# Experts' rows turned as float32r and as float32, and expert 0's row loads placed ahead of a branch

## The chip, the cores and the metric

One core of a Trainium2 chip runs the whole program. The metric is the device time in microseconds of one execution; the kernel before has a median of 955.91 us over two timed runs (955.81 and 956.01).

## What is computed

Three layers follow one another: attention with a gate (4 batches, 8 heads, 576 positions, 64 wide), a mixture of 8 experts with one expert per row (2304 rows of 512, 1024 hidden units), and a gated product of two matrices (1536 wide). The part that matters here is the second:

```python
N, D, E, F = (2304, 512, 8, 1024)
expert_idx = np.argmax(logits, axis=1)
...
for e in range(E):
    mask = expert_idx == e
    ...
    h = np.maximum(x[mask] @ w1[e], 0.0)
    out[mask] = gate_w[mask, None] * (h @ w2[e])
```

## The kernel before

Attention runs under a schedule made when the program is built, and its last tiles scatter their rows into a table `xs` in DRAM, one stretch per expert, with indirect DMAs from GpSimd. After that everything stands in the order in which the code issues it; every engine takes its instructions in that order.

Matrix products of float32 accuracy are made of three float32r products: an operand is split into a high half (`xh`, `hh`, the first half of a weight tile `w` or `v`), which is a cast, and a low half (`xl`, `hl`, the second half of the tile), which is the difference; high by high, low by high and high by low are added in PSUM. A weight tile `st` (128 x 1024) comes by SyncE's queue; `hi_op` casts it on ScalarE, `lo_op` subtracts on VectorE ("D") or GpSimd ("G"), 512 columns at a time.

The experts run in order of their size (`CAPS`, 352 to 272 rows; `ARMS` and `narrow` choose a column count of 256 or more by the true count). For expert `e` and each of 8 column blocks `f`, `products` issues 12 matmuls `h` (`hmm`), 12 matmuls `y` of the block before (`ymm`), the ReLU into `hh` on ScalarE and `hl` on VectorE. After the products of `f` = 3 to 6, `xtr(e + 1, f - 3)` turns a quarter of the next expert's rows: three 128x128 transposes into a PSUM bank `x` (two banks in turn), a cast to `xh` on ScalarE, a subtraction to `xl` on VectorE. Each turn also splits one weight tile and loads another (`wsplit2`, `wload2`), and takes one of the small jobs `m1` to `m5` out of `misc`. The rows of an expert come by `xload(e)` into a tile `xg` that has one buffer; `zfill(e)` first writes zeros into the unused rows of its stretch of `xs`. `yout` stores an expert's result `yt` through four buffers of the pool `mxp`, which also serves `g` in the second network.

Between attention and expert 0 stands a hand-over. Every engine reads a count `cov` and branches over a loop (`overflow`) that is for experts that have more rows than planned. TensorE runs warm-up matmuls of 512 columns (`idle(n)`, counts out of `WARM`), SyncE issues `xload(0)` behind the branch, which waits for all scattered rows, VectorE does two `lo_op`s each of tiles 4 and 5 and GpSimd two of tile 6, then `m1` and `m2` (ScalarE and VectorE), `zfill(1)`, three weight loads, and `xtr0` turns expert 0's rows: eight transposes (two row tiles for each of four quarters) and then four, each quarter in its own bank `y`, each followed by a cast and a subtraction.

Of the kernel before, what the change touches and what calls it, by code (L numbers as in the profile page):

```python
# [7 lines left out]
F32 = mybir.dt.float32  # L8
F32R = mybir.dt.float32r
# [4 lines left out]
ALU = mybir.AluOpType  # L14
# [20 lines left out]
PEND = (10, 1, 1)  # L35
WARM = (30, 84, 2, 0, 20, 10, 3)
LAT = 140.0
# [107 lines left out]
def moe_kernel(tc, q, k, v, s, emb, tau, w1, w2, wa, wb, wo, out, dbg=None):  # L145
    nc = tc.nc
# [35 lines left out]
    with left, right:  # L182
# [28 lines left out]
        base = rt.tile([128, E], F32, name="base")  # L211

        pmt = const.tile([128, N // 128, 2], F32, name="pmt")
        cumd = dram.tile([B * H, 64], F32, name="cumd")
# [24 lines left out]

        def slot_load(src):  # L240
            t = slot([128, 1024], F32, "st")
            d = t if len(src.shape) == 2 else t.rearrange("p (a c) -> p a c", a=src.shape[1])
            nc.sync.dma_start(out=d, in_=src)
            return t
# [44 lines left out]
        if True:  # L289
# [839 lines left out]
            def blank(eng, t, n):  # L1129
# [6 lines left out]
                out=ident, in_=onef, pattern=[[-1, 128]], compare_op=ALU.is_equal, fill=0.0, base=0, channel_multiplier=1  # L1136
            )
            nc.gpsimd.memset(mine, -1.0)
            for base_, x in ((0, 1), (31, -1)):
# [201 lines left out]
            hp = pool(right, "hp", 2, side="right")  # L1341
            mxp = pool(right, "mxp", 4, side="right")
            keep = pool(right, "keep", 1, side="right")
# [33 lines left out]
            def xtr0():  # L1377
                t = xhs[0] = [xhp.tile([128, 4, GT], F32R, name=x)[:, :, :CAPS[0]] for x in ("xh", "xl")]
                for a0, a1 in ((0, 256), (256, CAPS[0])):
                    for d in range(4):  # L1380
                        for a in range(a0, a1, 128):
                            nc.tensor.transpose(
                                out=yb[d][:, a:a + 128], in_=xgs[0][:, a // 128, 128 * d:128 * d + 128], identity=ident
                            )
                        nc.scalar.copy(out=t[0][:, d, a0:a1], in_=yb[d][:, a0:a1])
                        nc.vector.tensor_tensor(
                            out=t[1][:, d, a0:a1], in0=yb[d][:, a0:a1], in1=t[0][:, d, a0:a1].bitcast(F32), op=ALU.subtract
                        )

            def xtr(e, d):  # L1390
# [5 lines left out]
                for a in range(3):  # L1396
                    nc.tensor.transpose(  # L1397
                        out=pt[:, 128 * a:128 * a + 128], in_=xgs[e][:, a, 128 * d:128 * d + 128], identity=ident
                    )
                nc.scalar.copy(out=xh[:, d, :], in_=pt[:, :cap])  # L1400
                nc.vector.tensor_tensor(out=xl[:, d, :], in0=pt[:, :cap], in1=xh[:, d, :].bitcast(F32), op=ALU.subtract)

# [19 lines left out]

            def wload2():
                if loaded[0] < len(jobs):
                    key = jobs[loaded[0]][0]
                    stg[key] = slot_load(slot_src(who(key[0]), key[1]))
                    loaded[0] += 1
# [329 lines left out]

            wload2()
            idle(WARM[2])
            most = nc.values_load(cov[:1, 0:1], min_val=-CAP, max_val=N)  # L1760
            overflow()
            xload(0)
            cbase[1] = nc.sync.value_load(ci[:1, 1, 1:2], min_val=0, max_val=N)
            who(1)
            idle(WARM[6])
            count(0)
            for j in range(4, 7):
                for x in range(2):
                    lo_op("DG"[j == 6], wstate[j], slots[0, j], 512 * x, 512 * x + 512)
            for _ in range(2):  # L1770
                misc.pop(0)()
            zfill(1)
            for _ in range(3):
                wload2()
            xtr0()
            prev = None
# [105 lines left out]
```

## Time and profile before

| what | us |
|---|---|
| median of two timed runs | 955.91 |
| profiled execution, its own time | 953.78 |
| span of the profiled execution | 952.1 |
| TensorE busy (share of the span) | 917.8 (96%) |
| VectorE busy | 516.9 (54%) |
| ScalarE busy | 432.0 (45%) |
| GpSimd busy | 256.4 (27%) |

The span runs from the first to the last instruction; the profiled execution's own time is 1.7 us more. Attention takes about 258 us of it, the experts' matmuls run from about 272 to 490 us, the second network from there to the end. A share of busy time is an average over these stages; what a change in one of them is worth is read from that stage. PE in a row is TensorE's matmuls, PEld its weight loads, DVE VectorE, ACT ScalarE, POOL GpSimd, SPq SyncE's queue.

### The profile page before, as it was taken

The page shows a single profiled execution, that of the slowest core. Times are in us where ns is not written, and L with a number is a line of the kernel's source. Part 1 is how long each engine was busy: PE and PEld are TensorE (multiplying, and loading weights), DVE is VectorE, ACT ScalarE, POOL GpSimd, SP SyncE. Part 2 cuts the span into 40 slices and gives each one's busy share as a digit, 9 for nine tenths or more (in the row PEclk, how much of TensorE's full clock was granted, in tenths as well). Part 3 has the DMA queues.
Part 4 walks back from the last instruction along what each step waited for, and adds up shares of the span by engine and source line. Part 5 has one row for each costly group of instructions (what it writes and reads, how often), then busy time and mean ns, then how long its engine had stood idle before and what let it go on. Part 6 is the DMA issues. An engine that isn't in the chain of part 4 may idle for free.

```text
span 952.1 us, 17669 instructions
## 1 busy us (share of the span) xinstructions
PE 917.8 (96%) x6447; PEld 839.7 (88%) x6448; DVE 516.9 (54%) x1319; ACT 432.0 (45%) x1074; POOL 256.4 (27%) x308
## 2 busy tenths in 40 slices
PE   8998999999889999999999999999999999999996
PEld 7777878777669999999998999999999999999995
DVE  8788888798756343455678888732212222222112
ACT  6677888876645444455544434421211111121111
POOL 6122323256234333344303344632001001001001
PEclk9999999999999999999999999999999999999999
DMA  5774555526277667677736444412010010000000
GB/s 136 175 154 105 143 116 123 140 71 185 96 221 241 225 193 218 215 226 241 223 106 204 129 118 131 90 26 75 1 34 34 1 34 34 1 1 34 1 1 34
DMA packets 102259, 107.90 MB, mean 113 GB/s; under 512 B 58445, under 2 KB 72733, under 8 KB 102157
## 3 DMA queue, kind: packets, MB, share of 16 engines
q1 hardware_dynamic: 98573, 97.04, 36.0%
q0 software_dynamic: 3552, 9.46, 2.8%
q8 instruction: 65, 1.06, 0.5%
q14 instruction: 37, 0.30, 0.1%
q10 hardware_dynamic: 32, 0.04, 0.0%
HBM read 77.90 MB, written 20.44 MB: 103 GB/s over the span
## 4 chain that ended last, share of the span: by engine, by line
PE 68%; DMA 2%; DVE 0%; issue 0%; SPq 0%; POOLq 0%; ACT 0%; DVEq 0%; ACTq 0%
PE h L1643 16%; PE x L1643 16%; PE y L1664 14%; PE y L1578 10%; PE h L1553 10%; DMA xg<-xs 1%; PE x L1397 1%; PE x L1664 1%; PE h L1664 1%; DMA xs<-zrow 1%; DMA yt<-mx 0%; DVE xl L1631 0%; SPq L1372 0%; POOLq L1878 0%; DVE mx L1654 0%
## 5 line engine op out<-in xcount | busy, mean ns | idle before, releaser
L1654 DVE TENSOR_TENSOR mx<-x,mx 128x384 f32<-128x384 f32 x72 | 39.9, 555 | 225.1 <-PE x L1643 225.0
L1655 ACT CAST hh<-mx 128x384 fp32r<-128x384 f32 x71 | 36.4, 512 | 159.0 <-DVE mx L1654 159.0
L1649 ACT COPY mx<-h 128x384 f32<-128x384 f32 x72 | 34.5, 479 | 150.8 <-PE h L1643 149.8
L1683 POOL DMA_INDIRECT out_dram<-mx,pmt x18 | 17.6, 979 | 292.5 <-DVE mx L1682 223.2
L653 ACT ACTIVATE z<-z,mn 128x192 f32<-128x192 f32 (+3 forms) x128 | 78.2, 611 | 37.9 <-DVE mn L647 37.2
L1643 PE MATMUL h<-xh,w 128*128 128x384 f32 x288 | 79.8, 337 | 1.3 <-ACT mx L1649 1.3
L1643 PE MATMUL h<-xh,v 128*128 128x384 f32 x288 | 79.7, 337 | 0.0
L1643 PE MATMUL x<-xh,w 128*128 128x384 f32 x288 | 78.9, 334 | 0.0
L633 PE MATMUL st<-KS,QS 128*128 128x288 f32 (+3 forms) x160 | 58.7, 374 | 9.4 <-DVE mn L647 7.4
L756 PE MATMUL pt<-ident,z 128*128 128x128 f32 x448 | 63.5, 277 | 3.3 <-ACT pT L180 1.6
L281 POOL TENSOR_TENSOR w<-st,w 128x512 fp32r<-128x512 f32 (+1 forms) x43 | 47.1, 1101 | 68.1 <-ACT w L273 57.8
L647 DVE CUSTOM_DVE_ANT_0 z<-st,maskb 128x192 f32<-128x192 f32 (+3 forms) x128 | 58.7, 477 | 9.5 <-PE st L636 7.3
L1562 DVE SCALAR_TENSOR_TENSOR hl<-h,hh 128x288 fp32r<-128x288 f32 (+6 forms) x64 | 31.2, 487 | 58.8 <-ACT hh L1561 58.8
L1656 DVE TENSOR_TENSOR hl<-mx,hh 128x384 fp32r<-128x384 f32 x71 | 39.7, 559 | 41.1 <-ACT hh L1655 41.1
L800 PE MATMUL xa<-pT,vn 128*64 128x128 f32 x896 | 60.0, 278 | 1.9 <-ACT pT L180 1.6
L281 POOL TENSOR_TENSOR v<-st,v 128x512 fp32r<-128x512 f32 x32 | 43.2, 1353 | 62.5 <-ACT v L273 48.7
L1664 PE MATMUL y<-v,hh 128*128 128x512 f32 x192 | 59.8, 392 | 0.0
L756 PEld LDWEIGHTS pt<-ident,z 128*128 128x128 f32 x448 | 49.9, 141 | 11.0 <-ACT z L653 4.3
L1553 PE MATMUL h<-xh,v 128*128 128x256 f32 (+2 forms) x256 | 59.0, 304 | 0.0
L1578 PE MATMUL y<-hh,v 128*128 128x256 f32 (+2 forms) x256 | 58.0, 300 | 0.0
L1553 PE MATMUL h<-xh,w 128*128 128x288 f32 (+3 forms) x256 | 57.8, 302 | 0.0
L800 PEld LDWEIGHTS xa<-pT,vn 128*64 128x64 f32 x896 | 47.9, 137 | 11.0 <-issue 5.6
(308 smaller groups left out, 2520.0 us busy)
## 6 DMA issues: line engine op xcount, KB each, us to landing
st<-in_moe_w_dram SPq DMA_DIRECT2D x64, 512.0 KB
QS<-sp SPq DMA_DIRECT2D x62, 128.0 KB
st<-in_moe_w_a_dram SPq DMA_DIRECT2D x12, 512.0 KB
st<-in_moe_w_b_dram SPq DMA_DIRECT2D x12, 512.0 KB
st<-in_moe_w_out_dram SPq DMA_DIRECT2D x12, 512.0 KB
xg<-yt SPq DMA_DIRECT2D x6, 768.0 KB
xg<-xs SPq DMA_DIRECT2D x7, 512.0 KB
kn<-in_k_dram SPq DMA_DIRECT2D x24, 128.0 KB
```

What stands on the lines that cost most here:

```text
L281: e.tensor_tensor(out=o[:, 1, a:b], in0=t[:, a:b], in1=o[:, 0, a:b].bitcast(F32), op=ALU.subtract)
L633: nc.tensor.matmul(st[:m, :wp], lhsT=qs[:, h, s0 - 64:s0 - 64 + m], rhs=ks[:, h, c0:c0 + wp], start=True, stop=False)
L647: nc.vector.tensor_tensor_reduce(out=z[:m, h, c0:c0 + w], in0=st[:m, :w], in1=maskb[:m, S - kk + c0:S - kk + c0 + w], op0=ALU.add, op1=ALU ...
L653: nc.scalar.activation(out=z[:m, h, :kk], in_=z[:m, h, :kk], func=AF.Exp, scale=-1.0, bias=m1, accum_out=rsum[:m, tid(b, c), 2 * p + h:2 * ...
L756: nc.tensor.transpose(out=pt[:, 128 * x:128 * x + 128], in_=zs[i][:, h, a0:a0 + 128] if c else z0s[u % 2], identity=ident)
L800: nc.tensor.matmul(xa[64 * h:64 * h + 64, :m], lhsT=v_[:m, 2 * p + h, :], rhs=locs[i][bk, h], start=bk == 0, stop=bk == c,)
L1553: nc.tensor.matmul(ph[:, :n], lhsT=w[:, hl, 128 * f:128 * f + 128], rhs=mv[:, d, :n], start=k_ == 0, stop=k_ == 11,)
L1578: nc.tensor.matmul(ys[e][d][:, :n], lhsT=w[:, hl, c0 + 128 * d:c0 + 128 * d + 128], rhs=mv[:, :n], start=f == 0 and k_ == 0, stop=f == 7 a ...
L1643: nc.tensor.matmul(p, lhsT=w[:, hl, d, c0:c0 + 128], rhs=mv[:, d, :], start=d == 0 and k_ == 0, stop=d == 3 and k_ == 2,)
L1654: nc.vector.tensor_tensor(out=g, in0=pp[1], in1=g, op=ALU.mult)
L1656: nc.vector.tensor_tensor(out=gl, in0=g, in1=gh.bitcast(F32), op=ALU.subtract)
L1664: nc.tensor.matmul(ots[i][t], lhsT=st[:, 128 * t:128 * t + 128], rhs=w[:, hl, c0:c0 + 512], start=f == 0 and k_ == 0, stop=f == 11 and k_ ...
```

## The change

In `xtr`, the three transposes of a quarter are issued as float32r (rows and a cast identity `idr` taken as float32r), from which `xh` is cast as before; then three more transposes of the same rows are issued as float32 into the other bank `x`. VectorE copies the first result to SBUF (`c1`), subtracts it from the second (`c2`), subtracts `xh` from `c1`, and makes `xl` as `c2` times 1e12 plus that. In `xtr0` the 12 transposes are float32r only. `mxp` has five buffers in place of four.

In the hand-over, `xload(0)` comes before the warm-up and the branch, in the place of the load of weight tile (0, 7); all four warm-up matmuls stand ahead of the branch and none behind it. VectorE keeps the `lo_op`s of tile 4, GpSimd has those of 5 and 6; three small jobs are taken, ahead of GpSimd's `lo_op`s in the code; `xtr0` comes before `zfill(1)` and the weight loads; the load of tile (0, 7) now waits for the ninth transpose of `xtr0`, and two loads follow `zfill(1)` in place of three.

```diff
-WARM = (30, 84, 2, 0, 20, 10, 3)
+WARM = (30, 84, 4, 0, 20, 10, 0)
...
+        idr = const.tile([128, 128], F32R, name="idr")
...
-            nc.sync.dma_start(out=d, in_=src)
+            x = nc.sync.dma_start(out=d, in_=src)
+            if after:
+                tc.add_manual_dep(x.ins, after, DEP, reason="rows first")
...
+            nc.gpsimd.tensor_copy(out=idr, in_=ident)
...
-            mxp = pool(right, "mxp", 4, side="right")
+            mxp = pool(right, "mxp", 5, side="right")
...
-                            nc.tensor.transpose(
-                                out=yb[d][:, a:a + 128], in_=xgs[0][:, a // 128, 128 * d:128 * d + 128], identity=ident
+                            x = nc.tensor.transpose(
+                                out=yb[d][:, a:a + 128].bitcast(F32R), in_=xgs[0][:, a // 128, 128 * d:128 * d + 128].bitcast(F32R), identity=idr
...
+                        if a0 and d == 0:
+                            first = x.ins.name
+                return first
...
-                        out=pt[:, 128 * a:128 * a + 128], in_=xgs[e][:, a, 128 * d:128 * d + 128], identity=ident
+                        out=pt[:, 128 * a:128 * a + 128].bitcast(F32R), in_=xgs[e][:, a, 128 * d:128 * d + 128].bitcast(F32R), identity=idr
                     )
                 nc.scalar.copy(out=xh[:, d, :], in_=pt[:, :cap])
-                nc.vector.tensor_tensor(out=xl[:, d, :], in0=pt[:, :cap], in1=xh[:, d, :].bitcast(F32), op=ALU.subtract)
+                p2 = bank("x")
+                for a in range(3):
+                    nc.tensor.transpose(
+                        out=p2[:, 128 * a:128 * a + 128], in_=xgs[e][:, a, 128 * d:128 * d + 128], identity=ident
+                    )
+                c1, c2 = (mxp.tile([128, 512], F32, name="mx") for _ in range(2))
+                nc.vector.tensor_copy(out=c1[:, :cap], in_=pt[:, :cap])
+                nc.vector.tensor_tensor(out=c2[:, :cap], in0=p2[:, :cap], in1=c1[:, :cap], op=ALU.subtract)
+                nc.vector.tensor_tensor(out=c1[:, :cap], in0=c1[:, :cap], in1=xh[:, d, :].bitcast(F32), op=ALU.subtract)
+                nc.vector.scalar_tensor_tensor(
+                    out=xl[:, d, :], in0=c2[:, :cap], scalar=1e12, in1=c1[:, :cap], op0=ALU.mult, op1=ALU.add
+                )
...
-            wload2()
+            xload(0)
             idle(WARM[2])
             most = nc.values_load(cov[:1, 0:1], min_val=-CAP, max_val=N)
             overflow()
-            xload(0)
+            idle(WARM[6])
             cbase[1] = nc.sync.value_load(ci[:1, 1, 1:2], min_val=0, max_val=N)
             who(1)
-            idle(WARM[6])
             count(0)
-            for j in range(4, 7):
+            for x in range(2):
+                lo_op("D", wstate[4], slots[0, 4], 512 * x, 512 * x + 512)
+            for _ in range(3):
+                misc.pop(0)()
+            for j in (5, 6):
                 for x in range(2):
-                    lo_op("DG"[j == 6], wstate[j], slots[0, j], 512 * x, 512 * x + 512)
+                    lo_op("G", wstate[j], slots[0, j], 512 * x, 512 * x + 512)
+            turned = xtr0()
+            wload2(turned)
+            zfill(1)
             for _ in range(2):
-                misc.pop(0)()
-            zfill(1)
-            for _ in range(3):
                 wload2()
-            xtr0()
```

SyncE's queue in the hand-over. Before, behind the branch (its last row is the first one here): the row loads `xg`, two counts, the zero rows of expert 1 and then four weight tiles `st`; the load of tile (0, 7) stands ahead of the branch.

```order
L1704 UNCONDITIONAL_BRANCH
L1372 DMA xg<-xs 128x512 x2
L1372 DMA xg<-xs 96x512
L1763 TENSOR_LOAD ci
L1763 ISA x2
L1356 TENSOR_LOAD ci
L1356 ISA x2
L1257 ISA
L1257 DMA xs<-zrow 736x1x256
```

In the change, the same queue ahead of the branch, where `cov` is read (L1778):

```order
L244 DMA st<-in_moe_w_dram 128x2x512 x3
L1376 DMA xg<-xs 128x512 x2
L1376 DMA xg<-xs 96x512
L1778 TENSOR_LOAD cov
L1778 ISA x2
```

And behind the branch in the change:

```order
L1722 UNCONDITIONAL_BRANCH
L1781 TENSOR_LOAD ci
L1781 ISA x2
L1360 TENSOR_LOAD ci
L1360 ISA x2
L244 DMA st<-in_moe_w_dram 128x2x512
L1261 ISA
L1261 DMA xs<-zrow 736x1x256
```

The row loads moved from behind the branch to ahead of it, and the load of tile (0, 7) from ahead of it to behind it, in front of the zero rows.

VectorE behind the branch, before: the fill of `xg`'s unused rows, four `lo_op`s, `m1` and `m2`, and the first subtraction of `xtr0`.

```order
L1704 UNCONDITIONAL_BRANCH
L1368 MEMSET xg 32x512
L281 TENSOR_TENSOR w_4051<-st,w_4051 128x512 x2
L281 TENSOR_TENSOR w_4129<-st,w_4129 128x512 x2
L1479 TENSOR_SCALAR nr<-nr 128x20
L1480 RECIPROCAL nr<-nr 128x20
L1483 TENSOR_TENSOR lt<-lg,nr 128x160
L1484 TENSOR_REDUCE gm<-lt 128x20
L1485 TENSOR_TENSOR lt<-lt,gm 128x160
L1386 TENSOR_TENSOR xl<-y_4633,xh 128x256
```

The same place on ScalarE in the change, from the branch to the first casts of `xtr0`:

```order
L1722 UNCONDITIONAL_BRANCH
L1496 ACT_TABLE_LOAD
L1496 ACTIVATE nr<-ss 128x20
L1506 ACT_TABLE_LOAD
L1506 ACTIVATE lt<-lt 128x160
L1389 CAST xh<-y_4635 128x256
L1389 CAST xh<-y_4636 128x256
```

VectorE's list loses the fill (now ahead of the branch) and the `lo_op`s of tile 5, which GpSimd gets; on ScalarE the exponential of `m3` (L1506), which stood in the expert loop, now stands ahead of the first cast.

TensorE in the expert loop, where the first quarter of expert 1 is turned, in the change: the end of `y`, the turn, and the next `h`.

```order
L1596 MATMUL y_4638<-hl,w_4131 128x352
L1596 MATMUL y_4638<-hh,w_4131 128x352
L1555 UNCONDITIONAL_BRANCH
L1404 MATMUL x_5146<-idr,xg 128x128 x3
L1410 MATMUL x_5151<-ident,xg 128x128 x3
L1555 COMPARE_AND_BRANCH
L1571 MATMUL h_4633<-xh,w_3364 128x288
```

VectorE beside it, in the change, from one `hl` over the turn to the split of a weight tile:

```order
L1580 SCALAR_TENSOR_TENSOR hl<-h_4634,hh 128x352
L1414 COPY mx<-x_5146 128x368
L1555 UNCONDITIONAL_BRANCH
L1415 TENSOR_TENSOR mx<-x_5151,mx 128x368
L1416 TENSOR_TENSOR mx<-mx,xh 128x368
L1417 SCALAR_TENSOR_TENSOR xl<-mx 128x368
L284 TENSOR_TENSOR v_5161<-st,v_5161 128x512
```

Of the first list, before has the `ident` row alone, and of the second one subtraction `xl<-x,xh` in place of the four rows from L1414 to L1417; everything else in both lists stands where it stood.

## Rows read from the trace of the kernel before

**Rows 1.** The page's head: the profiled execution's span.
```profile
span 952.1 us, 17669 instructions
```
**Rows 2.** Busy time by windows: us, then PE, PEld, DVE, ACT, POOL; clock, DMA, GB/s.
```profile
280.00:290.00 10.00, 8.43 (x63) 7.99 (x63) 6.85 (x13) 6.77 (x14) 4.68 (x4) 1.00 1.05 355
...
360.00:370.00 10.00, 10.00 (x68) 10.00 (x67) 4.50 (x8) 5.16 (x11) 4.77 (x4) 1.00 0.66 202
```
**Rows 3.** Waits of PE from 271 to 490: total us, times, longest.
```profile
PE x L1397 <- DMA xg<-xs: 1.6, 2, 1.2
```
**Rows 4.** Chain of work, a turn of expert 5 (256 columns): start us, us, what.
```profile
429.69 0.33 PE x L1397 x3
430.01 1.44 PE h L1553 x12
431.45 1.44 PE y L1578 x12
```
**Rows 5.** The transposes' line: duration ns min/median/max, first and last start.
```profile
L1397 PE MATMUL x<-ident,xg x84: 270/272/331, 284.3 to 463.7; 128*128 128x128 f32 x84
```
**Rows 6.** Timeline of the hand-over: start us, us, engine, line, operation [idle before].
```profile
261.38 2.48 POOL L281 TENSOR_TENSOR w<-st,w 128x512 fp32r<-128x512 f32 x2 [1.75 <-POOLq L1704]
...
263.12 3.09 DVE L281 TENSOR_TENSOR w<-st,w 128x512 fp32r<-128x512 f32 x4
...
264.81 1.83 SPq L1372 DMA_DIRECT2D xg<-xs  x3
...
266.13 0.16 DVE L1479 TENSOR_SCALAR nr<-nr 128x20 f32<-128x20 f32 x1
...
267.35 0.32 DVE L1485 TENSOR_TENSOR lt<-lt,gm 128x160 f32<-128x160 f32 x1
...
269.68 2.48 ACT L1385 CAST xh<-y 128x256 fp32r<-128x256 f32 x8 [6.75 <-issue]
```
**Rows 7.** Timeline where the second network begins.
```profile
502.47 0.48 ACT L1649 COPY mx<-h 128x384 f32<-128x384 f32 x1 [1.07 <-DMA yt<-mx]
503.00 0.44 PE L1643 MATMUL h<-xh,w 128*128 128x384 f32 x1 [1.25 <-ACT mx L1649]
```
**Rows 8.** Timeline of PE: warm-up matmuls at the start, and ahead of the branch.
```profile
7.53 4.86 PE L174 MATMUL xa<-ones 128*128 128x128 bf16 x84
...
258.25 3.45 PE L174 MATMUL h<-w 128*128 128x512 f32 x4 [0.77 <-DVE jk L1301]
```
**Rows 9.** Windows of the hand-over; the third number from the end is the granted clock.
```profile
258.00:260.00 2.00, 1.75 (x2) 0.84 (x3) 1.68 (x13) 2.00 (x6) 1.32 (x2) 0.50 0.52 197
...
262.00:264.00 2.00, 0.00 (x0) 0.00 (x0) 1.37 (x2) 0.93 (x2) 1.86 (x2) 1.00 0.03 8
```
**Rows 10.** VectorE operations by line: duration ns min/median/max, first and last start.
```profile
L1401 DVE TENSOR_TENSOR xl<-x,xh x28: 442/466/542, 285.9 to 464.4; 128x288 fp32r<-128x288 f32 x8, 128x368 fp32r<-128x368 f32 x4, 128x344 fp32r<-128x344 f32 x4, 128x328 fp32r<-128x328 f32 x4
...
L178 DVE COPY mx<-y x16: 434/473/542, 301.9 to 498.0; 128x288 f32<-128x288 f32 x4, 128x352 f32<-128x352 f32 x2, 128x368 f32<-128x368 f32 x2, 128x344 f32<-128x344 f32 x2
...
L1656 DVE TENSOR_TENSOR hl<-mx,hh x71: 558/559/560, 495.3 to 934.8; 128x384 fp32r<-128x384 f32 x71
```
**Rows 11.** Timeline of expert 0: a GpSimd subtraction and a small VectorE operation.
```profile
286.95 1.31 POOL L281 TENSOR_TENSOR v<-st,v 128x512 fp32r<-128x512 f32 x1 [3.35 <-ACT v L273]
...
287.34 0.95 DVE L1492 TENSOR_SCALAR gm<-gm 128x20 f32<-128x20 f32 x1
```
**Rows 12.** Chain of work and timeline: loads of expert 0's rows, zero rows, expert 1's rows.
```profile
266.21 3.38 DMA xg<-xs
...
269.80 6.20 DMA xs<-zrow
...
276.11 0.39 SPq L1374 DMA_DIRECT2D xg<-xs  x1
...
285.00 0.33 PE L1397 MATMUL x<-ident,xg 128*128 128x128 f32 x1 [0.32 <-DMA xg<-xs]
```
**Rows 13.** Timeline of the start: GpSimd.
```profile
8.64 1.93 POOL L541 CAST KS<-KH 64x576 fp32r<-64x576 f32 x2 [1.81 <-ACT KH L408]
```

More of the change, by code (lines that the diff above doesn't have):

```diff
@@ L238, in slot, with slot_load @@
             return (spare[0] if spare and x < 62 and (x + 3) % 5 > 2 else stage).tile(shape, dtype, name=nm, tag="st")
-        def slot_load(src):
+        def slot_load(src, after=None):
             t = slot([128, 1024], F32, "st")
             d = t if len(src.shape) == 2 else t.rearrange("p (a c) -> p a c", a=src.shape[1])
-            nc.sync.dma_start(out=d, in_=src)
+            x = nc.sync.dma_start(out=d, in_=src)
+            if after:
+                tc.add_manual_dep(x.ins, after, DEP, reason="rows first")
             return t
@@ L1421, in ringpool, with wload2 @@
                 return ringa0 if nm in ("w0", "w1", "w2", "w3") else rings[nm] if nm in rings else ringa1[0] if nm[0] == "w" else rings[nm[0]]
-            def wload2():
+            def wload2(after=None):
                 if loaded[0] < len(jobs):
                     key = jobs[loaded[0]][0]
-                    stg[key] = slot_load(slot_src(who(key[0]), key[1]))
+                    stg[key] = slot_load(slot_src(who(key[0]), key[1]), after)
                     loaded[0] += 1
```

## The prediction

> **What bounds the kernel now.** The whole first: the profiled execution spans 952.1 us [rows 1] inside a run of 953.78 us; the two timed runs have the median 955.91. The sum below is made against 953.78, and the forecast is the median plus the same difference. The change touches three places, so I read each by the stage that holds it.
>
> The expert stage (about 272 to 490 us) comes first, by its windows and by TensorE's waits. TensorE is busy 10.00 of 10 us in the window from 360 to 370, VectorE 4.50, GpSimd 4.77 [rows 2], and in all of 271 to 490 TensorE waits 1.6 us, for one thing only: the rows of the second expert, `xg` [rows 3]. So what is added to TensorE's queue there is added to the time. The chain of work shows a turn of the loop: 12 matmuls of `h`, 12 of `y`, and where an expert's rows are turned, three transposes in 0.33 us [rows 4]. There are 84 such transposes, 28 turns [rows 5].
>
> The hand-over from attention to the experts (258 to 272 us) comes second, by the timeline of all engines [rows 6]; there nobody is full and a chain of waits sets the start. The turn of the page from experts to the second network (490 to 503 us) comes third: one wait of 1.25 us [rows 7].
>
> **Added transposes.** Each of the 28 turns gets three float32r transposes on top of the float32 ones: 84 instructions on an engine that has no gap. No row shows a 128-column float32r transpose. From below: 84 matmuls 128x128 in bf16, one pass over the columns, take 4.86 us, 0.058 each [rows 8]. From above: four rows of float32 matmul with 512 columns, which are two matmuls, take 3.45 us at a granted clock of 0.50 [rows 8, 9]; that is 1.73 us for 512 columns at half clock, 0.216 for 128 at full clock. Between them lie the float32 transpose itself (0.33/3 = 0.11) and the narrowest float32r matmul, 256 columns in 1.44/12 = 0.120 [rows 4]. The instruction is nearest to these two and to the one-pass row, so I take the middle of 0.058 and 0.120: 0.09. 84 x 0.09 = 7.6 us; ends 4.9 and 18.1. The 12 transposes of expert 0 that change their type gain or lose 12 x 0.02 = 0.2 inside waits: nothing.
>
> [...]
>
> **Added VectorE work.** A turn had one subtraction of 0.466 us; it now has a copy out of PSUM (0.473), a subtraction out of PSUM (0.466), one within SBUF and a scalar-tensor-tensor within SBUF (0.559 for 384 columns, so about 0.45 here) [rows 10]: 1.84 us, 1.4 more, 39 us in all. The cover is TensorE's own turn. The shortest turn is 1.44 + 1.44 + 0.33 [rows 4] + 0.27 = 3.5 us; VectorE's is 0.47 (`hl`) + 1.84 + 0.69 (`lo_op`) = 3.0. It fits, but two of the new operations read SBUF alone. Such operations wait for GpSimd: a tensor_scalar of 128x20 took 0.95 us while a GpSimd subtraction ran from 286.95 to 288.26 [rows 11]. One such wait a turn (up to 1.3) makes 4.3. Behind the new operations on VectorE stand `lo_op` and the next `hl`; `y` of a turn reads `hl` only after the next `h`, which leaves about 1.7 us. Also both transposes of a turn now take both `x` banks, so the next turn waits for this turn's reads, with about as much room. Four such turns in a row per expert, then none: I put 0.3 us, ends 0 and 10 (rival below).
>
> **Row loads in front of the branch.** Before, SyncE sat behind the branch and issued the three loads of expert 0's rows from 264.81 to 266.64 [rows 6], and the last took 3.38 us [rows 12]. The scattered rows were there earlier: DMA share is 0.03 from 262 to 264 [rows 9]. Now the loads go out near 261.6 and land near 266.4, where the warm-up matmuls, all four ahead of the branch, are over. So the transposes could be done near 266.7. But the first cast of `xh` (269.68, call it X) now stands behind m3's exponential on ScalarE, and that behind m1 and m2 on VectorE, which ran 266.13 to 267.68 [rows 6]. VectorE is rid of two `lo_op`s; GpSimd gets two more: four of 1.24 us from 261.38 [rows 6]. VectorE's own two and m1 and m2 want the same port and must wait in between (one waited in the row of 3.09 us for four, where 0.69 each is 2.76). If VectorE waits as little as before, X is 266.9; if it waits a GpSimd operation before each, 269.4. I take 268.9.
>
> The page "SBUF — State Buffer" of the Trainium skill, section "Who interferes with whom", says that VectorE with two SBUF inputs and a GpSimd instruction that reads SBUF exclude each other for a whole instruction. The rows of 0.95 us and 3.09 us agree; by this rule the moved `lo_op`s speak against the change, and X would be at the late end.
>
> Then the stall moves on. In before, the zero rows went out at 269.80 (X + 0.1) and landed 6.2 us later; the rows of expert 1, issued 276.11, landed at 285.0 (X + 15.3), and TensorE stood [rows 12]. Now the weight tile (0,7), loaded long before, is issued behind the ninth transpose (X + 1.3: a cast, a subtraction and the transpose, some 0.4 each), with the zero rows behind it (X + 2.1). At 355 GB/s [rows 2] its 524 KB take 1.5 us: zero rows land at X + 9.8, and expert 1's rows, behind three tiles instead of four (8.9 - 1.5 = 7.4), at X + 17.2. With X = 268.9 that is 286.1 against 285.0: 1.1 us lost, whatever expert 0 gained before it. Ends: X = 266.9, 0.9 gained; X = 269.4, 1.6 lost. With no warm-up behind the branch a stretch of half clock, such as the one at 258 to 260 [rows 9], may fall on expert 0's first matmuls; each us of it loses half a us, and up to 3 us are hidden by the same stall.
>
> **A fifth `mx` buffer.** At 501.4 ScalarE waits 1.07 us for a store `yt<-mx` to free the buffer of the second `g`, and TensorE 1.25 us behind it [rows 7]. With five buffers that `g` takes the first `g`'s, read long ago: 1.1 gained; ends 0 and 1.25. Next late there is nothing within 1 us.
>
> **`idr`.** One GpSimd copy at the start; GpSimd then idles 1.81 us before its next urgent work [rows 13]: nothing; uncovered it would be 0.5.
>
> **Sum.** 7.6 + 0.3 + 1.1 - 1.1 = 7.9. 953.78 + 7.9 = 961.7 for the profiled run, 955.91 + 7.9 = 963.8 for the median.
>
> **Rivals.**
> - Narrow float32r at four passes (0.216): 963.8 - 7.6 + 18.1 = 974.3. For it: no float32r row in this trace is narrower than 256 columns, and `s_item` pads to that. Against: the float32 transpose at 0.11 is at half of its matmul's price already. Chance 0.11.
> - VectorE becomes the bound in the four turns: 4.3 against 3.5 us, 4 x 0.8 = 3.2 less 1.7 of room = 1.5 per expert, seven experts 10.5: 963.8 - 0.3 + 10.5 = 974.0. For it: the 0.95 us row. Against: GpSimd's operation can lie beside `hl`, copy and first subtraction (1.4 us), which read PSUM. Chance 0.08.
> - Not slower: the early row loads pay in full. X = 266.0 starts expert 0 3.7 us earlier, and expert 1's rows come in time, so the 1.6 us stall goes too: 5.3 + 1.1 = 6.4 gained, against 4.9 for transposes at 0.058: 955.91 - 1.5 = 954.4. It decides if a transpose costs under 6.4/84 = 0.076. Against it stands the amount of data ahead of those rows. Chance 0.05.
>
> **How the numbers follow.** My forecast has 0.76: from 4.9 with X early (955.91 + 4.9 - 0.9 - 1.1 = 958.8) to 0.120 with X late (955.91 + 10.1 + 1.6 = 967.6). The range 958.5 to 972 leaves out the four-pass case (0.11), the not-slower case (0.05) and half of the VectorE case (0.04). 2%, about what a measurement of this kernel can tell from no change, is 19.1 us: slower means over 975.0, which half of the first and half of the second rival reach: 0.09. Faster by 2% none of the cases gives: 0.01. Within 2%: 0.90.
>
> **What would show it.** The new transposes' row in the chain of work: 0.27 for three says my price, 0.17 the lower, 0.65 the upper. TensorE's waits from 271 to 490 must name `xg` alone; a wait for `mx`, `xl` or `hl` on VectorE is the second rival. The first `xh` cast and the landing of expert 1's rows say whether the early loads paid: 268.9 and 286.1 by my working. The wait at 503 should be gone. I am wrong if any transposes' price lies outside the bounds, or if TensorE's waits in the expert stage pass 4 us.

## The result, and the profile after

The changed kernel takes 970.03 us (median of two runs, 968.77 and 971.29) against 955.91: ratio 1.0148, 95% interval 1.0124 to 1.0173. That is 14.1 us more, inside the range and on the forecast side, but 6.2 us above the value of 963.8. The profiled execution is the one of 968.77.

The page's head after, which answers to [rows 1]:

```profile
span 967.1 us, 17950 instructions
```

What TensorE waits for from 272 us, just ahead of expert 0's first `h`, to 506, where the second network begins (us in total, times, longest), which answers to [rows 3]:

```profile
PE y L1596 <- DVE hl L1580: 5.1, 6, 1.3
PE y L1386 <- DVE xl L1390: 2.8, 1, 2.8
PE x L1404 <- DMA xg<-xs: 0.8, 2, 0.5
PE y L1596 <- ACT hh L1579: 0.5, 1, 0.5
```

Before, `xg` stood there alone. (`y L1386`, 2.8 us, is the ninth transpose of `xtr0`, which belongs to the hand-over.) Now `hl` on VectorE comes first. Windows with turns in them say why; busy us of PE, PEld, DVE, ACT, POOL, then clock, DMA share and GB/s. Before, in expert 6:

```profile
450.00:460.00 10.00, 10.00 (x86) 10.00 (x85) 4.80 (x9) 5.26 (x12) 3.45 (x4) 1.00 0.70 241
```

After:

```profile
360.00:370.00 10.00, 10.00 (x72) 9.96 (x71) 9.49 (x14) 5.34 (x11) 4.38 (x3) 1.00 0.43 142
420.00:430.00 10.00, 10.00 (x83) 9.79 (x81) 9.62 (x15) 4.93 (x12) 4.64 (x4) 1.00 0.56 185
```

VectorE was busy 4.80 of 10 us among turns (the window of [rows 2] from 360 to 370, with 4.50, holds no turn); it is busy 9.49 and 9.62 now, with 14 and 15 operations in place of 9. What fills it are the durations of the new operations. By line (busy us, mean ns of one), from 272 to 506:

```profile
L1417 DVE SCALAR_TENSOR_TENSOR xl<-mx 128x288 fp32r<-128x288 f32 (+5 forms) x28 | 25.3, 904 | 1.0
L1416 DVE TENSOR_TENSOR mx<-mx,xh 128x288 f32<-128x288 f32 (+5 forms) x28 | 25.1, 897 | 1.0
...
L1415 DVE TENSOR_TENSOR mx<-x,mx 128x288 f32<-128x288 f32 (+5 forms) x28 | 13.5, 483 | 3.1 <-DVE mx L1414 0.5
L1414 DVE COPY mx<-x 128x288 f32<-128x288 f32 (+5 forms) x28 | 13.3, 477 | 9.3 <-ACT xh L1407 8.5
```

The two that read PSUM cost what [rows 10] say, 0.48 us. The two that read SBUF alone cost 0.90, nearly twice. The timeline of two turns of expert 6, first VectorE, then GpSimd:

```profile
476.59 0.44 DVE L1415 TENSOR_TENSOR mx<-x,mx 128x272 f32<-128x272 f32 x1
477.07 1.07 DVE L1416 TENSOR_TENSOR mx<-mx,xh 128x272 f32<-128x272 f32 x1
478.17 0.44 DVE L1417 SCALAR_TENSOR_TENSOR xl<-mx 128x272 fp32r<-128x272 f32 x1
478.54 0.68 DVE L284 TENSOR_TENSOR v<-st,v 128x512 fp32r<-128x512 f32 x1
479.14 0.45 DVE L1580 SCALAR_TENSOR_TENSOR hl<-h,hh 128x288 fp32r<-128x288 f32 x1
...
480.51 1.06 DVE L1416 TENSOR_TENSOR mx<-mx,xh 128x272 f32<-128x272 f32 x1
...
481.97 1.78 DVE L284 TENSOR_TENSOR v<-st,v 128x512 fp32r<-128x512 f32 x1
483.67 0.45 DVE L1580 SCALAR_TENSOR_TENSOR hl<-h,hh 128x288 fp32r<-128x288 f32 x1
```
```profile
476.54 1.30 POOL L284 TENSOR_TENSOR v<-st,v 128x512 fp32r<-128x512 f32 x1 [2.14 <-DVE mx L1414]
479.98 1.29 POOL L284 TENSOR_TENSOR v<-st,v 128x512 fp32r<-128x512 f32 x1 [2.14 <-DVE mx L1414]
481.78 1.42 POOL L284 TENSOR_TENSOR v<-st,v 128x512 fp32r<-128x512 f32 x1 [0.51 <-ACT v L276]
```

The first L1416, 0.44 us of work, takes 1.07: it ends at 478.14, just behind GpSimd's subtraction, which runs to 477.84; `lo_op` at 481.97 takes 1.78 us instead of 0.68 beside GpSimd's of 481.78. VectorE's list in such a turn has no gap: it runs at the pace of TensorE (3.44 us), and by the rows of both engines each `hl` starts some 1.9 us after its `hh` is done, where before it was 0.03. There TensorE still waits for nothing. The `lo_op` of 1.78 us makes the next `hl` 3.1 us late, and TensorE waits 1.2 us in the first step of the next expert. So the price of four full turns is paid once, behind them.

**Where the 14 us lie.** I read the start of the first warm-up matmul ahead of the branch, of the first `h` of experts 0 and 1, and of the first matmul of the second network, and subtract:

| stretch | before | after | difference |
|---|---|---|---|
| start to first warm-up matmul | 258.25 | 259.93 | +1.7 |
| warm-up to expert 0's step f = 4 | 26.87 | 28.85 | +2.0 |
| from there to expert 1's first `h` | 13.73 | 16.06 | +2.3 |
| experts 1 to 7 | 190.89 | 200.90 | +10.0 |
| second network | 462.36 | 461.34 | -1.0 |

These are the two profiled executions, which differ by 15.0 us. The first and the last line will turn out not to belong to the change. The steps of TensorE within an expert give the rest: a turn of experts 1 to 7 is longer by 0.234 us, 24 of them 5.6 us; the other 4.4 stand in the first steps of experts 1, 5, 6 and 7, behind their predecessors' turns (2.88 to 4.21 us in expert 6, 2.88 to 4.13 in expert 7). In expert 0, step 5 goes from 3.50 to 5.31.

### The profile page after: what moved, and what is told of

Same layout as the page of the kernel before. It is cut to its first block, busy times and chain, and to the rows that moved or that the text cites. A ratio compares the mean times of both kernels' runs of the same rounds, so it can differ in the third digit from the quotient of the medians.

```text
span 967.1 us, 17950 instructions
## 1 busy us (share of the span) xinstructions
PE 927.0 (96%) x6529; PEld 849.1 (88%) x6530; DVE 579.7 (60%) x1401; ACT 432.1 (45%) x1074; POOL 264.0 (27%) x311
## 4 chain that ended last, share of the span: by engine, by line
PE 48%; DVE 2%; issue 0%; ACT 0%; POOLq 0%; DVEq 0%; ACTq 0%
PE h L1661 15%; PE x L1661 15%; PE y L1682 14%; PE y L1596 1%; PE h L1571 1%; PE x L1682 1%; PE h L1682 1%; DVE mx L1416 0%; DVE v L284 0%; DVE xl L1649 0%; DVE mx L1415 0%; POOLq L1898 0%; DVE hl L1580 0%; DVE mx L1414 0%; DVE cv L269 0%
## 5 line engine op out<-in xcount | busy, mean ns | idle before, releaser
L284 POOL TENSOR_TENSOR w<-st,w 128x512 fp32r<-128x512 f32 (+1 forms) x45 | 52.2, 1169 | 68.9 <-ACT w L276 39.6
L284 POOL TENSOR_TENSOR v<-st,v 128x512 fp32r<-128x512 f32 x32 | 45.3, 1420 | 67.4 <-ACT v L276 38.2
L1596 PE MATMUL y<-hh,w 128*128 128x288 f32 (+3 forms) x256 | 56.7, 296 | 0.5 <-ACT hh L1579 0.5
```

The costliest lines, as they stand in the source:

```text
L284: e.tensor_tensor(out=o[:, 1, a:b], in0=t[:, a:b], in1=o[:, 0, a:b].bitcast(F32), op=ALU.subtract)
L1596: nc.tensor.matmul(ys[e][d][:, :n], lhsT=w[:, hl, c0 + 128 * d:c0 + 128 * d + 128], rhs=mv[:, :n], start=f == 0 and k_ == 0, stop=f == 7 a ...
```

## The experiments

The runs were made on three chips on which the kernel before takes 954.87, 971.19 and 971.16 us, so each is compared by its ratio to the kernel before on its own chip, and by the stretches of the experts in the table above, which hardly depend on the chip: experts 1 to 7 take 190.89 us in the kernel before and 190.90 in the one with the fifth buffer alone, on another chip. (Attention and the second network do depend on it: 266.67 and 470.90 us there, for 258.25 and 462.36.)

**The transposes alone.**

```diff
                 nc.vector.tensor_tensor(out=xl[:, d, :], in0=pt[:, :cap], in1=xh[:, d, :].bitcast(F32), op=ALU.subtract)
+                p2 = bank("x")
+                for a in range(3):
+                    nc.tensor.transpose(out=p2[...].bitcast(F32R), in_=xgs[e][...].bitcast(F32R), identity=idr)
```

> The kernel before with the 84 float32r transposes added in the turns and nothing else (their result is read by no one). Theory A (a float32r transpose costs 0.078 us, as the longer turns of the changed kernel say; the rest of the 14 us comes from VectorE): 84 x 0.078 = 6.6, so 962.5 us. Rival B (the extra VectorE work is hidden, as I forecast, and the transposes carry the whole 14 us, 0.17 each): about 970 us. The forecast's own price of 0.09 gives 963.5. If the float32r identity at the start delays attention, the first warm-up ahead of the branch starts near 259.9 instead of 258.25 here too.

962.75 us, ratio 1.0071 (1.0054 to 1.0088): +7.9. Experts 1 to 7 take 197.64 us, 6.75 more, 0.281 in each of 24 turns, 0.094 for a transpose. The turn on TensorE in this kernel and in the changed one:

```profile
437.13 0.49 PE L1399 MATMUL x<-ident,xg 128*128 128x128 f32 x3
437.37 0.46 PE L1406 MATMUL x<-idr,xg 128*128 128x128 f32 x3
437.66 0.35 PE L1560 MATMUL h<-xh,v 128*128 128x256 f32 x1
```
```profile
441.09 0.37 PE L1404 MATMUL x<-idr,xg 128*128 128x128 f32 x3
441.30 0.52 PE L1410 MATMUL x<-ident,xg 128*128 128x128 f32 x3
441.57 0.37 PE L1571 MATMUL h<-xh,v 128*128 128x256 f32 x1
```

From start to start three float32r transposes take 0.21 to 0.29 us and three float32 ones 0.24 to 0.27, by which comes first. With float32r ahead a turn is 0.234 longer (0.078 for each), with float32 ahead 0.281. Theory A holds, and the forecast's 0.09 lies between the two. No wait for VectorE appears in the turns; rival B, 0.17 each, is out.

**The VectorE work alone.**

```diff
-            mxp = pool(right, "mxp", 4, side="right")
+            mxp = pool(right, "mxp", 5, side="right")
...
-                nc.vector.tensor_tensor(out=xl[:, d, :], in0=pt[:, :cap], in1=xh[:, d, :].bitcast(F32), op=ALU.subtract)
+                c1, c2 = (mxp.tile([128, 512], F32, name="mx") for _ in range(2))
+                nc.vector.tensor_copy(out=c1[:, :cap], in_=pt[:, :cap])
+                nc.vector.tensor_tensor(out=c2[:, :cap], in0=pt[:, :cap], in1=c1[:, :cap], op=ALU.subtract)
+                nc.vector.tensor_tensor(out=c1[:, :cap], in0=c1[:, :cap], in1=xh[:, d, :].bitcast(F32), op=ALU.subtract)
+                nc.vector.scalar_tensor_tensor(out=xl[:, d, :], in0=c2[:, :cap], scalar=1e12, in1=c1[:, :cap], op0=ALU.mult, op1=ALU.add)
```

> The kernel before with the four VectorE operations in the place of one subtraction, both subtractions out of PSUM taking the one float32 transposition, and the fifth mx buffer; no transposes are added. Theory A (VectorE is late for y in the turns, because the operations within SBUF wait for GpSimd): some 5.6 us of waits of TensorE for hl, less 1.0 for the buffer, 960.5 us; the waits may be a little less than in the changed kernel or more, since TensorE's own turn is 0.24 us shorter: 959 to 963. Rival B (that work is hidden): 954.9 us.

965.89 us, ratio 1.0108 (1.0091 to 1.0125): +11.0, more than theory A said, and more than the transposes. TensorE's waits from 270 to 505, and the two operations within SBUF at the commonest width:

```profile
PE y L1584 <- DVE hl L1568: 4.3, 6, 1.7
PE h L1559 <- DVE xl L1405: 2.0, 4, 0.7
```
```profile
L1404 DVE TENSOR_TENSOR mx<-mx,xh 128x288 f32<-128x288 f32 x8 | 7.8, 969 | 0.3
L1405 DVE SCALAR_TENSOR_TENSOR xl<-mx 128x288 fp32r<-128x288 f32 x8 | 7.6, 954 | 0.3
```

Experts 1 to 7 lose 6.5 us to VectorE here, against 4.4 in the changed kernel, and the stretch from the warm-up to expert 1 loses 3.8: TensorE's turn is 0.23 us shorter than there, so VectorE has less time. The two additions are therefore not a sum: 7.9 and 11.0 alone would be 18.9, and together, with the hand-over, they are 14.1. The reading is that each turn's transposes give VectorE time that it needs; no run varies that time alone.

**The same work, but no operation that reads SBUF alone.** The changed kernel with the difference of the two transpositions left in PSUM:

```diff
-                nc.vector.tensor_tensor(out=c2[:, :cap], in0=p2[:, :cap], in1=c1[:, :cap], op=ALU.subtract)
-                nc.vector.tensor_tensor(out=c1[:, :cap], in0=c1[:, :cap], in1=xh[:, d, :].bitcast(F32), op=ALU.subtract)
+                nc.vector.tensor_tensor(out=p2[:, :cap], in0=p2[:, :cap], in1=c1[:, :cap], op=ALU.subtract)
+                nc.vector.tensor_tensor(out=c1[:, :cap], in0=pt[:, :cap], in1=xh[:, d, :].bitcast(F32), op=ALU.subtract)
                 nc.vector.scalar_tensor_tensor(
-                    out=xl[:, d, :], in0=c2[:, :cap], scalar=1e12, in1=c1[:, :cap], op0=ALU.mult, op1=ALU.add
+                    out=xl[:, d, :], in0=p2[:, :cap], scalar=1e12, in1=c1[:, :cap], op0=ALU.mult, op1=ALU.add
```

> The changed kernel with the same four VectorE operations a turn, but none of them reads SBUF alone: the difference of the two transpositions is written back into PSUM, and xh is subtracted from the PSUM tile instead of its copy. Theory A1 (those operations wait for GpSimd's subtractions): the waits of TensorE for hl go from 5.1 to under 1 us and the longer first steps after the turns with them, 970.0 - 5 = 965 us. Rival A2 (it is the amount of VectorE work, not whom it waits for): 970 us, or a little more if PSUM is dearer than SBUF. Rival B (VectorE plays no part): 970 us.

965.8 us, ratio 1.0100 (1.0083 to 1.0117) against 1.0148. The same two lines and the wait for `hl`:

```profile
L1416 DVE TENSOR_TENSOR mx<-x,xh 128x288 f32<-128x288 f32 (+5 forms) x28 | 13.5, 483 | 1.0
L1417 DVE SCALAR_TENSOR_TENSOR xl<-x,mx 128x288 fp32r<-128x288 f32 (+5 forms) x28 | 13.5, 483 | 1.0
```
```profile
PE h L1571 <- issue: 1.4, 2, 1.0
...
PE y L1596 <- DVE hl L1580: 0.4, 1, 0.4
```

The operations are as many and of the same size, and take 0.483 us where they took 0.90. (By the second measurement of the changed kernel, 1.0127, the times alone would not tell the two apart; the traces do.) Every first step behind the turns is back at its old length (expert 6: 2.88), and experts 1 to 7 take 196.98 us, 3.9 less. The stretch from the warm-up to expert 1, though, got 1.7 us longer (46.58 for 44.91), part of it in a wait that the profile puts down to nothing it shows (`issue`); that stays open.

**The VectorE work without GpSimd's subtractions.** The kernel with the VectorE work alone, and GpSimd's half of each split left out:

```diff
                     for x in range(2):
                         hi_op("A", t, o, 512 * x, 512 * x + 512)
-                        lo_op("DG"[x], t, o, 512 * x, 512 * x + 512)
+                        if x:
+                            nc.gpsimd.memset(o[:, 1, 512:].bitcast(F32), 0.0)
+                        else:
+                            lo_op("D", t, o, 0, 512)
```

> The kernel with the VectorE work alone (e2_vector_work), in which GpSimd's half of each weight split in the expert stage is left out: a GpSimd memset writes zeros into the low half of the second 512 columns of every tile, so the low-half products of those columns are missing. The number of VectorE operations is that of e2_vector_work. Theory A1 (VectorE's operations within SBUF wait for GpSimd's subtractions): the 6.3 us of waits of TensorE for hl and xl go, 956 us. Rival A2 (the amount of VectorE work): stays at 966 us.

Ratio 1.0004 (0.9988 to 1.0019): no difference from the kernel before. VectorE's two operations, and TensorE's waits for `hl`:

```profile
L1405 DVE SCALAR_TENSOR_TENSOR xl<-mx 128x288 fp32r<-128x288 f32 (+5 forms) x28 | 13.6, 484 | 1.0
L1404 DVE TENSOR_TENSOR mx<-mx,xh 128x288 f32<-128x288 f32 (+5 forms) x28 | 13.5, 483 | 1.0
```
```profile
PE y L1587 <- DVE hl L1571: 0.9, 1, 0.9
```

Here nothing of VectorE's list is changed, and the operations still read SBUF alone; without GpSimd's subtractions beside them they take 0.483 us, and experts 1 to 7 191.16 us (before 190.89). A GpSimd memset of the same size, 0.53 us, doesn't hold them up: in 6 of the 28 turns memsets lie beside the two operations, which keep their length. Of this run and the one ahead of it, one takes the reading of SBUF away and the other the neighbour, and each ends the waits for `hl` but for one of under 1 us. Theory A1 is shown, A2 is out.

**The hand-over alone.** The kernel before with the diff's `WARM`, the place of `xload(0)`, the `lo_op`s, the small jobs, `xtr0` ahead of `zfill(1)` and the load that waits for the ninth transpose; float32 transposes, four buffers.

> The kernel before with the hand-over of the change alone: the row loads and all warm-up matmuls ahead of the branch, three small jobs, GpSimd's four low halves, the load of tile (0, 7) between the ninth transposition and the zero rows. No float32r transposition, four mx buffers. My forecast's step says +1.1 us, from expert 1's rows, which land 17.2 us after the first xh cast instead of 15.3, less what that cast comes earlier. By the traces of the changed kernel and of the one with float32r turns, counted from the first warm-up matmul to the fifth step of expert 0, it is +1.7 to +2.5. Theory A: +1.7 to +2.5. Rival B (the early row loads pay, the loss seen there belongs to the float32r transpositions): 0 to -1 us.

Ratio 1.0010 (0.9992 to 1.0028), so -0.8 to +2.7 us. From the warm-up to step 4 of expert 0 it takes 29.42 us, against 25.95 and 26.87 in two executions with the old hand-over. TensorE's waits in step 3 of expert 0, and the end of that step:

```profile
PE y L1583 <- ACT hh L1566: 1.6, 1, 1.6
...
PE y L1583 <- DVE hl L1567: 0.4, 1, 0.4
```
```profile
295.31 0.44 PE L1583 MATMUL y<-hh,w 128*128 128x288 f32 x1
295.55 0.67 PE L1402 MATMUL x<-ident,xg 128*128 128x128 f32 x3
```

TensorE does not wait for expert 1's rows here. It waits for `hh` and `hl`: ScalarE stood idle 4.7 us for a weight tile (until 289.22), and the ReLU into `hh` comes behind the four casts that follow. So this run shows what the new hand-over costs, but not by the path that the forecast names. During that wait the clock falls to the lower of its two levels (granted 0.5, 1.2 of 2.4 GHz, from 292.5 to 295.9), which costs 1.7 us; without it the stretch would be 27.7 us, 0.8 to 1.8 more than with the old hand-over, and with it it takes 2.5 to 3.5 more. Every one of these stretches speaks against rival B, a gain of up to 1, though the timing does not exclude it; the size stays uncertain by more than a us.

**The zero rows first.** The changed kernel with the old order on SyncE's queue:

```diff
-            wload2(turned)
             zfill(1)
+            wload2(turned)
```

> The changed kernel with the zero rows of expert 1 issued ahead of the load of weight tile (0, 7), as they stood before the change. Theory A (expert 1's rows are what expert 0 waits for, and they stand behind the zero rows): the zero rows land about 1.5 us earlier and expert 1's rows about 2 us, to 15.3 us after the first xh cast, and the half clock on expert 0's first matmuls (1.6 us in two steps) is still hidden: 1.5 to 2 us faster than the changed kernel, 968.2 us. Rival B (the half clock on expert 0's first matmuls sets its end): no gain, 970 us.

Ratio 1.0126 (1.0099 to 1.0153); the changed kernel has 1.0148, and 1.0127 in a second measurement on another chip (below), so the time tells no gain. The trace does: warm-up to step 4 takes 26.22 us instead of 28.85 and 28.11 (two executions of the changed kernel), and neither `hh` nor the rows of expert 1 are waited for any more ahead of the first turn:

```profile
289.79 0.30 PE L1596 MATMUL y<-hh,w 128*128 128x288 f32 x1
289.93 0.37 PE L1404 MATMUL x<-idr,xg 128*128 128x128 f32 x3
```

Of the 2.6 us that this gives, 0.7 go again in steps 4 and 5, where VectorE is late: expert 1 begins 42.99 us after the warm-up, instead of 44.91. The half clock on expert 0's first matmuls (its first step still takes 3.01 us instead of 1.67) doesn't keep the gain away: theory A, by the trace.

**Both mended.** The changed kernel with no operation that reads SBUF alone and the zero rows first, beside the changed kernel as it is.

> The changed kernel with the two losses that I did not forecast, or too small, taken away together: no VectorE operation of a turn reads SBUF alone (as in e3_from_psum), and the zero rows go out ahead of tile (0, 7) (as in e7_zeros_first). Theory: the losses are independent, so 4.2 and 2.1 us less than the changed kernel; what is left over the kernel before is the transposes, 28 turns of 0.23 to 0.28, 6.6 to 7.8 us: ratio 1.0075 (1.006 to 1.009), the changed kernel in the same call at 1.0148. Rival: with VectorE on time the rows of expert 1 or the half clock take the gain back, and it stays at 1.010 or above.

> The changed kernel as it is, beside the next one on the same chip. Theory: the ratio to the kernel before is 1.0148 again, within its interval of 1.0124 to 1.0173.

1.0080 (1.0055 to 1.0106) and 1.0127 (1.0091 to 1.0163). The second was expected at 1.0148 and lies near the lower end of the interval given for it, 1.0124 to 1.0173. What is left with both mended is 0.8%, 7.6 us of 955, where 0.75% was expected. Experts 1 to 7 take 196.50 us, 5.6 over the kernel before, which is the 24 turns and nothing else. In expert 0 steps 4 and 5 are longer still (5.93 and 5.28 for 3.5), but not by VectorE: no wait for `hl` is left there. TensorE waits 1.6 us, just ahead of step 5, for nothing that the profile shows, and behind that wait it runs at half clock from 298.7 to 302.1. So the ratio of 1.0075 came out right with a part that I had not in it, and the two losses are not shown to be independent.

**The fifth buffer alone** (4 to 5 in the kernel before).

> The kernel before with five mx buffers in place of four and nothing else. Theory A (the wait of 1.25 us at the start of the second network stood in one execution by chance; two kernels with four buffers do not have it): no difference that can be measured, ratio 1.000, and no wait for mx there. Rival B (my forecast's step): 1.1 us faster, ratio 0.9988.

Ratio 1.0003 (0.9985 to 1.0022): theory A. No wait for `mx` is there, but neither is one in the kernel with the transposes alone and in that with the hand-over alone, which have four buffers. In the former, ScalarE's copy follows at once where [rows 7] had 1.07 us:

```profile
510.83 0.62 ACT L1474 CAST w<-cv 128x512 fp32r<-128x512 f32 x1 [0.71 <-DVE cv L267]
511.36 0.47 ACT L1656 COPY mx<-h 128x384 f32<-128x384 f32 x1
```

The wait in the trace of before stood in that one execution.

**float32r only.** The changed kernel without the float32 transposes and the three VectorE operations that go with them:

> The changed kernel without the float32 transposes of the turns and without the three VectorE operations that go with them: one float32r transposition, one cast, one subtraction. Everything else (hand-over, fifth buffer, identity) is as changed. Theory A: against the kernel before the turns get 84 x (0.109 - 0.078) = 2.6 us shorter, the fifth buffer gives 1.0, the hand-over with its half-clock first matmuls loses about 1.5 on expert 0, and attention 1.7 if its late end comes with the change: 955.9 - 2.6 - 1.0 + 1.5 + 1.7 = 955.5 us, 953.8 without the last. Rival B (a float32r transpose at 0.17 in place of 0.109): 84 x 0.06 = 5 us more in the turns, 961 us.

956.14 us, ratio 1.0010 (0.9999 to 1.0021). Experts 1 to 7 take 189.52 us, 1.4 less than before, 0.057 a turn: 1.6 for 28 turns, where 2.6 was expected, since a float32r transpose costs 0.09 alone in a turn and not 0.078. The hand-over takes it back, with 43.39 us from the warm-up to expert 1's first `h` against 40.60. Rival B, 5 us more, is out. So I put that saving on the old hand-over:

```diff
-                        out=pt[:, 128 * a:128 * a + 128], in_=xgs[e][:, a, 128 * d:128 * d + 128], identity=ident
+                        out=pt[:, 128 * a:128 * a + 128].bitcast(F32R), in_=xgs[e][:, a, 128 * d:128 * d + 128].bitcast(F32R), identity=idr
```

(and the same in `xtr0`, with `idr` and five buffers).

> The kernel before with float32r in place of float32 transpositions (in the turns and for expert 0) and five mx buffers; the hand-over stays as it was before. Theory A: 0.057 us less in each of 28 turns, 1.6, and 1.0 for the wait at the start of the second network if the fifth buffer is what ends it: 2.6 us faster than the kernel before, ratio 0.9973. Rival B (that wait was a chance of one execution, since the kernel with the transposes added and four buffers doesn't have it): 1.6 us faster, ratio 0.9983. If float32r saves nothing: 1.000.

Ratio 0.9971 (0.9953 to 0.9989): the interval lies below 1, so this is a little faster than the kernel before. The traces account for 1.4 us in experts 1 to 7 (189.52 again); from the warm-up to expert 1's first `h` it takes 39.84 us, which is no gain against the 39.69 of the kernel with the fifth buffer alone. The interval holds 1.6 (rival B) as well as 2.6 us (theory A); the run of the fifth buffer alone speaks for rival B.

## Why the forecast was right in side and range, and where it was not

**Added transposes: 7.6 forecast, 6.6 measured** (28 x 0.234). The price between the bounds was the right choice: 0.078 each with float32r first, 0.094 with float32 first, 0.09 forecast. The row named as the sign, 0.27 for three, came out as 0.27 where float32r transposes stand alone between `y` and `h` (3.15 us a turn less 2.88); in the changed kernel itself the three add 0.234, between that sign and the lower one of 0.17. The page "TensorE: Matmul & The Clock Gate" of the Trainium skill, section "Back-to-back issue gap", gives 56 ns for 128 columns as the gap of a single matmul, and about 81 ns for each in a stream where every matmul has its own weight load. The transposes here have their own weight loads, and 0.078 and 0.094 us agree with the second figure. By it an estimate of this term would be 84 x 0.081 = 6.8 us. The four-pass rival is out.

**Added VectorE work: 0.3 forecast, 6.0 measured.** This is the step that failed: 4.4 us behind the turns of experts 0, 4, 5 and 6, and 1.6 in expert 0 itself (2.3 less three turns of 0.234). The four durations were near enough (0.48 each without the neighbour, 1.93 us a turn for 1.84), and the wait was seen and even priced: "one such wait a turn", 1.3 us, makes 4.3 us against TensorE's 3.5. What was wrong is the sentence that set it aside, that GpSimd's operation can lie beside `hl`, the copy and the first subtraction out of PSUM. It could, but nothing makes it. GpSimd's line (busy us, mean ns, then idle us and what the profile says ended them):

```profile
L284 POOL TENSOR_TENSOR v<-st,v 128x512 fp32r<-128x512 f32 x32 | 45.3, 1420 | 67.4 <-ACT v L276 38.2 <-DVE mx L1415 15.8 <-PE h L1571 6.0
```

The profile names several instructions. ScalarE ahead of the subtraction of 476.54:

```profile
474.98 0.39 ACT L1407 CAST xh<-x 128x272 fp32r<-128x272 f32 x1 [1.24 <-PE x L1404]
475.26 1.15 ACT L276 CAST v<-st 128x512 fp32r<-128x512 f32 x2
```

Its casts of the weight tile end at 476.41, and from 280 us on 55 of GpSimd's 56 subtractions start 0.08 to 0.13 us behind such an end; in the kernel before, where VectorE has no such copy and subtraction, all 55 do. So ScalarE's cast releases them. It stands behind the cast of `xh`, and VectorE's copy and first subtraction run at nearly the same time: so GpSimd starts just ahead of the two operations within SBUF. In the turn of 476 us some 0.5 us of GpSimd's 1.30 do lie beside the subtraction out of PSUM; the rest is waited out. In 27 of the 28 turns one of these two is stretched to 0.88 us or more, never both. Together they carry (0.897 + 0.904 - 2 x 0.483) x 28 = 23 us of waiting on VectorE; some 6 of them reach TensorE. The page "SBUF — State Buffer" of the Trainium skill, section "Who interferes with whom", gives the rule for it: a VectorE instruction with two SBUF inputs contends with a GpSimd instruction that reads SBUF. The two rows of 0.90 and both runs without the meeting agree with it. [rows 11], which the prediction counts for this rule, is no case of it: that tensor_scalar has one input in SBUF (and took 0.95 us all the same).

**The rival on VectorE** had the right mechanism, at a chance of 0.08, and a price of 10.5, nearly twice what came. It took VectorE's turn to be longer than TensorE's, 4.3 against 3.5, and the delay to grow from turn to turn. In the trace the delay of `hl` stays between 1.4 and 2.0 us within the four turns of experts 1 to 6, up to the last `lo_op`; TensorE's own turn had grown by 0.23 us, and VectorE just keeps up. Experts 2, 3 and 4, whose predecessors' turns last 4.1 to 4.4 us, begin without loss. What tips it over in the others is the `lo_op` of 1.78 to 1.80 us behind the fourth turn of experts 0, 4, 5 and 6, where GpSimd's next subtraction starts 0.13 to 0.28 us ahead of it; behind that of experts 1 to 3 the `lo_op` is first, and takes 0.68 or 0.69.

**Row loads in front of the branch: 1.1 forecast, 1.7 measured** (2.0 to step 4, less 0.23 for the turn that lies in it). With the second execution of either hand-over in place of the first it is 1.0 to 2.7, so the size is loose. The steps held in the main. Counted from the warm-up, the first `xh` cast was forecast 10.65 us later (268.9) and came at 10.94; expert 1's last rows were to land 17.2 us behind the cast and were there after 17.5. In the changed kernel:

```profile
263.11 5.94 POOL L284 TENSOR_TENSOR w<-st,w 128x512 fp32r<-128x512 f32 x4 [1.82 <-ACT w L276]
...
264.48 3.42 DVE L284 TENSOR_TENSOR w<-st,w 128x512 fp32r<-128x512 f32 x2 [1.15 <-DVEq L1722]
...
267.83 1.25 DVE L1497 TENSOR_SCALAR nr<-nr 128x20 f32<-128x20 f32 x1
...
270.87 2.52 ACT L1389 CAST xh<-y 128x256 fp32r<-128x256 f32 x8
...
272.99 0.66 SPq L1261 DMA_DIRECT2D xs<-zrow  x1
```

Against [rows 6], VectorE's two `lo_op`s take 3.42 us where four took 3.09, and `m1`'s first operation 1.25 where it took 0.16: the late end of what I allowed for them. So the cast comes late although the rows are there at 268.15, and the load of (0, 7) keeps the zero rows back. What the forecast did not have is a second wait in step 3, of 0.5 us for `hh` and 0.4 for `hl`, ahead of the 0.8 for expert 1's rows: there too ScalarE stands idle for a weight tile (3.6 us, until 281.96), with `hh` behind its casts. In this trace the rows come last and set the end of the step; in the kernel with the hand-over alone `hh` and `hl` do. The half clock (0.50 in the windows from 270 to 276, falling while TensorE waits 2.8 us for `xl`) costs expert 0's first two steps 1.6 us. It fell where I had put it and was hidden, as the kernel with the zero rows first shows by giving its gain in spite of it.

**A fifth `mx` buffer: -1.1 forecast, 0 measured.** The wait was gone after, as forecast, and the trace pair shows -1.0; but two kernels with four buffers lack it too, and the timing of the buffer alone shows nothing. I took one wait of one execution, for a store to land, as a property of the kernel.

**`idr`: 0.** Attention ends 1.7 us later in the trace after, but not by `idr`: on one chip the first warm-up matmul starts at 260.39 in the kernel with the VectorE work alone, which has no `idr`, and at 260.09 to 260.32 in three kernels that have it. The rest is chance of the execution, or the chip.

**Sum.** 6.6 + 6.0 + 1.7 + 0 = 14.3, against 14.1 between the medians; the second measurement has some 12 (1.27%), so agreement to 0.2 is chance. The transposes were 1.0 too dear, the hand-over 0.6 and the buffer 1.1 too cheap, and VectorE carries 5.7 of the 6.4. The increase forecast, 7.9, is little more than half of what came, and the range held only because its upper end contained half of that rival. By the sign that the prediction itself names, waits of TensorE over 4 us in the expert stage, its account of that stage was wrong: they are 6.4 us (5.1 + 0.8 + 0.5), most of them for `hl`.

## What to carry to other kernels

Where operations of two engines exclude each other, don't ask whether they could lie apart; ask what releases each, and if the same events do, price one wait in every turn. Keeping one operand in PSUM made that wait go away at the same count of operations. A wait that one profiled execution shows once is worth a second execution before it enters a sum.

## What was not expected of the hardware

A 128-column float32r transpose is hardly cheaper than a float32 one: 0.09 us against 0.11 us, three in a turn between other matmuls. Their weight loads take 140 ns, as the float32 ones' do (141; PEld and PE of the line, duration ns min/median/max):

```profile
L1404 PEld LDWEIGHTS x<-idr,xg x84: 138/140/144, 287.7 to 478.1; 128*128 128x128 f32 x84
L1404 PE MATMUL x<-idr,xg x84: 220/228/281, 287.7 to 478.1; 128*128 128x128 f32 x84
```

Whether the loads set the pace stays open: the second and third float32r transpose of a turn start 60 and 65 ns behind the one before, less than a load takes, so the loads overlap. A scalar-tensor-tensor with two inputs in SBUF waits for GpSimd's subtraction just as a tensor-tensor does (954 and 969 ns at 288 columns, for 458 without), while a GpSimd memset of 128 x 512 beside them, met in 6 turns, costs them nothing.
